# Relu out of zeroed PSUM rows and positions in eight transfers in the prologue; the fold of two weight matrices and two more units moved to the end of the pair loop

## The chip, the cores and the metric

One core of one Trainium2 chip. The metric is device time in microseconds (us), the median of several executions. The kernel before takes 2534.7 us (median of the six runs measured beside the changed kernel, 2533.2 to 2537.5; 2536.1 over the first three of them, which the prediction uses).

The engines are called by their names or by the profile's: TensorE is PE, VectorE is DVE, ScalarE is ACT, GpSimd is POOL, SyncE is SP; SPq and ACTq are the transfers that SyncE and ScalarE issue.

## The reference, cut to what matters

```python
# x, v: (4, 12544, 128); pos_emb: (12544, 64); w1: (64, 64); w2: (64, 128)
h_filt = (np.maximum(pos_emb @ w1, 0.0) @ w2) * np.exp(-0.01 * pos)[:, None]
y = causal convolution along the sequence of (x * v) with h_filt     # by an FFT of 2 * 12544
attn = x * y
# feed-forward on all 4 * 12544 rows; moe_w1..3: (128, 768), moe_w_out: (768, 128)
h = np.maximum(np.maximum(attn @ moe_w1, attn @ moe_w2), attn @ moe_w3)
out = h @ moe_w_out
```

The kernel takes the FFT as matrix products: first stages over "units" of channels (transpose, matmul against a small table; 32 units a batch), then second and inverse stages over 45 pairs of frequencies. The first maxout weight is taken out of the maximum: `max(a, b, c) = a + max(0, b - a, c - a)`, and the `a` part becomes one matrix, `lin = w1 w_out`, built by six "folds".

## The kernel before: the parts that the change and the argument touch

In time order: a prologue (positions, relu, filter's first stage, batch 0's units), a loop over the 45 pairs for batch 0, its drain, then 4 x 32 feed-forward tiles of six hidden blocks each. Beside the tiles of one batch runs the convolution of the next, dealt out over that batch's 192 hidden blocks ("slots").

```python
    def mlp_out(i):                      # prologue: relu times window, four operations a group
        ps = hidden.pop(i)
        v = ps[:].rearrange("n (r t f) -> n r f t", r=2, t=8)
        for h in range(2):
            n = slice(64 * h, 64 * h + HH)
            for r in range(2):
                nc.vector.scalar_tensor_tensor(
                    out=hs[n, :, r, 8 * i:8 * i + 8], in0=v[n, r], scalar=0.0,
                    in1=winr[n, r, None, 8 * i:8 * i + 8].to_broadcast([HH, FO, 8]),
                    op0=ALU.max, op1=ALU.mult)
# ... (cut)
    def conv_steps(b, done, lag):        # where each step of the next batch goes, in slots
        # ... (cut)
        per_pair = 172 / (NK + 0.95 * (NU - done))
        for u in range(done, NU, 2):
            s = (u - done) * 0.95 * per_pair + 6
            # ... (cut: load, product, transposes and first-stage groups of unit u)
        s0 = int((NU - done) * 0.95 * per_pair) + 7
        for g in range(NK):
            s = s0 + int(g * per_pair)
            at(s - 6, g_load, g)
            at(s + lag[4], g_third, b, g)      # lag = (1, 2, 3, 4, 5)
            at(s, g_second, g)
            at(s + lag[0], g_butterfly, g)
            at(s + lag[1], g_swap, g)
            at(s + lag[1], g_re, g)
            at(s + lag[2], g_im, g)
            at(s + lag[3], g_unfold, g)
# ... (cut)
    def up(i, f):                        # one hidden block: pa -> ScalarE relu, pb -> VectorE max
        rhs = gs[i][:]
        h = hp.tile([P, N], FP32, tag="hid", name="hid")
        pa = hps.tile([P, 512], FP32, tag="hps", name="pa")     # pa and pb share 2 buffers
        halves_mm(pa[:, 0:N], w_sb[1][:, f * P:(f + 1) * P], rhs, True, True)
        nc.scalar.activation(h[:], pa[:, 0:N], Relu)
        pb = hps.tile([P, 512], FP32, tag="hps", name="pb")
        halves_mm(pb[:, 0:N], w_sb[2][:, f * P:(f + 1) * P], rhs, True, True)
        nc.vector.tensor_tensor(out=h[:], in0=h[:], in1=pb[:, 0:N], op=ALU.max)
        return h
# ... (cut)
    EARLY = 4                            # units of batch 1 that the pair loop takes
    for s in range(NK + 3):
        # ... (cut: third, second, swap, filter, products of the pairs in flight)
        if folded is not None:
            folded()
            folded = None
        if 2 <= s < 2 + NF:
            folded = fold(s - 2)         # transpose, copy; the matmul follows a step later
    nc.scalar.copy(lin[:], pl[:, 0:D])
# ... (cut)
            beside = conv_steps(b + 1, EARLY if b == 0 else 0, (1, 2, 3, 4, 5))
```

## Time and profile before

| Stage of the kernel before, from its trace | us |
|---|---|
| start to the first loop step (prologue) | 129.1 |
| loop and drain, to the first tile's matmul | 198.8 |
| tiles of batch 0, beside the convolution of batch 1 | 580.0 |
| tiles of batch 1 | 587.5 |
| tiles of batches 2 and 3 | 1038.8 |
| span | 2534.1 |

A batch is counted from the first matmul of its first tile to that of the next batch.

### The profile page before, as it was taken

How to read it: one execution, taken by the hardware profiler on the slowest of the kernel's cores; microseconds unless marked ns; L12 is line 12 of the kernel's file. 1: busy time of each engine (PE TensorE's matmuls, PEld its weight loads, DVE VectorE, ACT ScalarE, POOL GpSimd, SP SyncE). 2: the span in 40 equal slices, each digit the busy share in tenths (PEclk: the TensorE clock that was granted, in tenths of full speed). 3: DMA queues.
4: the chain of work that ended last, by engine and by line, in shares of the span. 5: the costliest groups of instructions: out<-in, count | busy, mean ns of one | idle time of the engine just before them, and what ended most of it. 6: DMA issues, size and time to landing. Idle time of an engine off the chain costs nothing. (4 is left out here: it accounts for less than half of the span.)

```text
span 2534.1 us, 62487 instructions
## 1 busy us (share of the span) xinstructions
PE 2490.4 (98%) x26369; PEld 1512.8 (60%) x26369; DVE 1269.3 (50%) x2512; ACT 1041.5 (41%) x1976; POOL 68.5 (3%) x121
## 2 busy tenths in 40 slices
PE   7999999999999999999999999999999999999999
PEld 6988755565655555656566556655666654444444
DVE  5578833346666633336666733334766642222222
ACT  1688823334444423334444433333544432222222
POOL 2022200000000000000000000000000000000000
PEclk8999999999999999999999999999999999999999
DMA  6778854458787644457888834446888842222221
GB/s 137 196 215 273 251 115 107 95 143 227 211 226 211 174 105 96 100 134 181 229 215 229 224 91 107 101 95 182 222 235 223 231 115 52 62 56 56 59 53 35
DMA packets 428462, 384.51 MB, mean 152 GB/s; under 512 B 291358, under 2 KB 338197, under 8 KB 428053
## 3 DMA queue, kind: packets, MB, share of 16 engines
q1 hardware_dynamic: 305216, 290.84, 45.9%
q10 hardware_dynamic: 117653, 74.73, 10.1%
q0 software_dynamic: 5312, 14.95, 2.1%
q8 instruction: 206, 3.38, 0.6%
q14 instruction: 75, 0.61, 0.1%
HBM read 295.73 MB, written 84.67 MB: 150 GB/s over the span
## 5 line engine op out<-in xcount | busy, mean ns | idle before, releaser
L472 DVE TENSOR_TENSOR hid<-hid,pb 128x392 f32<-128x392 f32 x768 | 431.5, 562 | 775.1 <-PE pb L126 671.6
L469 ACT ACTIVATE hid<-pa 128x392 f32<-128x392 f32 x768 | 382.4, 498 | 713.5 <-PE pa L126 653.4
L126 PE MATMUL pa<-gt,w_sb 128*64 128x392 f32 x3072 | 641.0, 496 | 13.0 <-ACT hid L469 11.5
L126 PE MATMUL pb<-gt,w_sb 128*64 128x392 f32 x3072 | 636.1, 493 | 1.0 <-DVE hid L472 1.0
L126 PE MATMUL ops<-hid,wo_sb 128*64 128x392 f32 x3072 | 635.7, 492 | 0.1
L126 PEld LDWEIGHTS pb<-gt,w_sb 128*64 128x64 f32 x3072 | 217.7, 136 | 290.3 <-issue 206.4
L126 PEld LDWEIGHTS ops<-hid,wo_sb 128*64 128x64 f32 x3072 | 219.7, 137 | 286.2 <-issue 285.5
L126 PEld LDWEIGHTS pa<-gt,w_sb 128*64 128x64 f32 x3072 | 192.5, 137 | 150.1 <-issue 99.5
L135 PEld LDWEIGHTS ps<-f,uT 98*64 98x64 f32 x4096 | 183.7, 138 | 61.7 <-issue 58.2
L377 DVE TENSOR_TENSOR xt<-xt,ht 128x512 f32<-128x512 f32 x180 | 124.4, 691 | 186.1 <-ACT xs L372 124.9
L126 PEld LDWEIGHTS yps<-f,zt 90*64 90x64 f32 x4096 | 188.5, 136 | 48.0 <-issue 45.6
L126 PEld LDWEIGHTS ps<-ab,wt 128*64 128x64 f32 x2880 | 165.6, 137 | 55.5 <-issue 31.4
L400 ACT COPY zs<-ps 128x512 f32<-128x512 f32 x180 | 105.7, 587 | 225.1 <-PE ps L126 215.2
L135 PE MATMUL ps<-f,uT 98*64 98x90 f32 x4096 | 195.5, 242 | 1.3 <-ACT zs L400 0.7
L126 PE MATMUL yps<-f,zt 90*64 90x98 f32 x4096 | 195.3, 247 | 0.6 <-DMA zt<-zd 0.6
L126 PE MATMUL ps<-ab,wt 128*64 128x128 f32 x2880 | 190.3, 274 | 3.9 <-DVE ab L388 3.0
L126 PE MATMUL ps<-spec,wt 128*64 128x128 f32 x2880 | 187.8, 273 | 0.0
L126 PEld LDWEIGHTS ps<-spec,wt 128*64 128x64 f32 x2880 | 164.9, 137 | 17.5 <-issue 17.5
L460 DVE TENSOR_TENSOR gt<-yps,xT 128x392 f32<-128x392 f32 x128 | 72.5, 566 | 161.0 <-PE yps L126 143.7
L371 ACT ACTIVATE xs<-xt 64x512 f32<-64x512 f32 x180 | 113.1, 628 | 79.8 <-DVE xt L152 47.9
L139 ACT COPY spec<-ps 128x360 f32<-128x360 f32 (+1 forms) x128 | 69.9, 546 | 168.2 <-PE ps L135 167.9
L388 DVE TENSOR_TENSOR ab<-xt 128x256 f32<-128x256 f32 x360 | 135.7, 418 | 1.6
(67 smaller groups left out, 1592.7 us busy)
## 6 DMA issues: line engine op xcount, KB each, us to landing
wt<-wt_const SPq DMA_DIRECT2D x135, 512.0 KB, 4.7
ht<-hd SPq DMA_DIRECT2D x270, 256.0 KB, 5.7
zd<-zs ACTq DMA_DIRECT2D x180, 256.0 KB, 4.9
zt<-zd SPq DMA_DIRECT2D x128, 360.0 KB, 5.9
ut<-in_xr_dram SPq DMA_DIRECT2D x128, 196.0 KB, 3.7
ut<-in_vr_dram SPq DMA_DIRECT2D x128, 196.0 KB, 4.0
xT<-in_x_dram SPq DMA_DIRECT2D x512, 49.0 KB, 4.2
out_dram<-ot ACTq DMA_DIRECT2D x128, 196.0 KB, 3.5
```

The costliest lines, as they stand in the source:

```text
L126: nc.tensor.matmul(out[64 * h:64 * h + 64], lhsT[:, 64 * h:64 * h + 64], rhs, start=start, stop=stop, skip_group_check=True)
L135: nc.tensor.matmul(ps[64 * c:64 * c + 64, 256 * i + r * N1:256 * i + (r + 1) * N1], a[:, r, :], table[:, c * N1:(c + 1) * N1], start=(i % ...
L139: copy(dst, ps[:].rearrange("p (s m) -> p s m", m=256)[:, :, 0:2 * N1].rearrange("p s (r k) -> p k r s", r=2))
L371: nc.scalar.mul(xs[0:64], xt[64:128], -1.0)
L377: nc.vector.tensor_tensor(out=xt[:], in0=xt[:], in1=hts[g][:, 0], op=ALU.mult)
L388: nc.vector.tensor_tensor(out=ab[:, :, q, :], in0=y[:, :, 0, :], in1=y[:, :, 1, :], op=op)
L400: nc.scalar.copy(zs[:].rearrange("p k f -> p (k f)"), ps[:])
L460: nc.vector.tensor_tensor(out=g[:], in0=ps[:, 0:N], in1=xTs.pop(i)[:].rearrange("d p n -> d (p n)"), op=ALU.mult)
L469: nc.scalar.activation(h[:], pa[:, 0:N], Relu)
L472: nc.vector.tensor_tensor(out=h[:], in0=h[:], in1=pb[:, 0:N], op=ALU.max)
```

## The change

Its intent: let the positions land sooner, halve VectorE's relu work (one operation over 105 rows in place of two over 41 and 41, with the rows between zeroed in PSUM), take the six folds out of loop steps that they made longer, and let the loop do two more units of batch 1, so that fewer are left beside the feed-forward tiles. The diff, cut to its core:

```diff
-    nc.gpsimd.memset(hs[32:64].rearrange("n f r t -> n (f r t)"), 0.0)
+    pms = [fps.tile([P, 1024], FP32, name=f"pm{i}", bufs=1) for i in range(2)]
+    for pm in pms:
+        nc.vector.memset(pm[32:64], 0.0)
 # ... (cut: positions in eight transfers on two queues; first units ahead of the raw weights)
-        for _ in range(10):
+        for _ in range(16):                      # warm-up rounds
 # ...
     def mlp_out(i):
-        ps = hidden.pop(i)
-        v = ps[:].rearrange("n (r t f) -> n r f t", r=2, t=8)
-        for h in range(2):
-            n = slice(64 * h, 64 * h + HH)
-            for r in range(2):
-                nc.vector.scalar_tensor_tensor(
-                    out=hs[n, :, r, 8 * i:8 * i + 8], in0=v[n, r], scalar=0.0,
-                    in1=winr[n, r, None, 8 * i:8 * i + 8].to_broadcast([HH, FO, 8]),
-                    op0=ALU.max, op1=ALU.mult)
+        v = pms[i % 2][0:64 + HH].rearrange("n (r t f) -> n r f t", r=2, t=8)
+        for r in range(2):
+            nc.vector.scalar_tensor_tensor(
+                out=hs[:, :, r, 8 * i:8 * i + 8], in0=v[:, r], scalar=0.0,
+                in1=winr[:, r, None, 8 * i:8 * i + 8].to_broadcast([64 + HH, FO, 8]),
+                op0=ALU.max, op1=ALU.mult)
 # ... (cut)
-    EARLY = 4
+    EARLY = 6
+    loads = dict(zip((NK - 16, NK - 14, NK - 12, NK - 9, NK - 8, NK - 4), range(EARLY)))
+    muls = dict(zip((NK - 13, NK - 11, NK - 10, NK - 5, NK - 3, NK - 1), range(EARLY)))
+    turns = {NK - 9: 0, NK - 4: 2}
     for s in range(NK + 3):
 # ...
-        if folded is not None:
-            folded()
-            folded = None
-        if 2 <= s < 2 + NF:
-            folded = fold(s - 2)
+        # (cut: loads, products and transposes of units from these tables)
+        if NK <= s < NK + 2:
+            for v in range(4):
+                u_first(2 * (s - NK) + v // 2, v % 2, nc.scalar.copy)
+    for f in range(NF):
+        folded = fold(f)
+        if f == 0:
+            u_turn(4)
+            u_turn(5)
+        folded()
     nc.scalar.copy(lin[:], pl[:, 0:D])
+    for u in (4, 5):
+        for h in range(2):
+            u_first(u, h)
 # ... (cut: the first-stage groups beside the first tile's loads go)
```

`conv_steps` isn't in the diff. It reads `EARLY` as its `done`.

More of the change, by code (lines that the diff above doesn't have):

```diff
@@ L224 @@
     sml = fin.enter_context(tc.tile_pool(name="sml", bufs=1))
-    fps = fin.enter_context(tc.tile_pool(name="fps", bufs=4, space=PSUM))
+    mps = ExitStack()
+    fps = mps.enter_context(tc.tile_pool(name="fps0", bufs=4, space=PSUM))
     specH = pin.tile([P, N1, 2, FO], FP32, name="specH")
@@ L244 @@
     nc.vector.memset(win[:], 0.0)
-    nc.gpsimd.memset(hs[32:64].rearrange("n f r t -> n (f r t)"), 0.0)
+    pms = [fps.tile([P, 1024], FP32, name=f"pm{i}", bufs=1) for i in range(2)]
+    for pm in pms:
+        nc.vector.memset(pm[32:64], 0.0)
     for h in range(2):
         nc.scalar.dma_start(w1_sb[64 * h:64 * h + 64], w1[:, :])
-        (nc.scalar if h else nc.sync).dma_start(
-            pos[64 * h:64 * h + 64], posT[:, h * HH * P:(h + 1) * HH * P])
+    cuts = (0, 11, 21, 31, HH)
+    for j, (lo_, hi_) in enumerate(zip(cuts, cuts[1:])):
+        for h in range(2):
+            (nc.scalar if (h + j) % 2 else nc.sync).dma_start(
+                pos[64 * h:64 * h + 64, lo_ * P:hi_ * P],
+                posT[:, (h * HH + lo_) * P:(h * HH + hi_) * P])
     for h in range(2):
@@ L262, in warm_up @@
     def warm_up():
-        ps = fps.tile([P, 1024], FP32, tag="cv", name="pw")
-        for _ in range(10):
+        ps = fps.tile([P, 1024], FP32, tag="cv", name="pw", bufs=2)
+        for _ in range(16):
             halves_mm(ps[:, 0:256], warm[:, 0:P], warm[:], True, True)
     def window_back():
-        pw = fps.tile([P, 1024], FP32, tag="cv", name="pw")
+        pw = fps.tile([P, 1024], FP32, tag="cv", name="pw", bufs=2)
         nc.tensor.transpose(pw[:, 0:64 + HH], win[:], eye[0:64 + HH, 0:64 + HH])
@@ L278, in window_back @@
                           w2_in[lo_:lo_ + FO].rearrange("f (g c) -> f c g", c=GC), m)
-    hidden = {}
     def mlp_in(i):
-        ps = fps.tile([P, 1024], FP32, tag="cv", name="pm")
+        ps = pms[i % 2]
         for r in range(2):
@@ L292, in mlp_in @@
                         skip_group_check=True)
-        hidden[i] = ps
     def mlp_out(i):
-        ps = hidden.pop(i)
-        v = ps[:].rearrange("n (r t f) -> n r f t", r=2, t=8)
-        for h in range(2):
-            n = slice(64 * h, 64 * h + HH)
-            for r in range(2):
-                nc.vector.scalar_tensor_tensor(
-                    out=hs[n, :, r, 8 * i:8 * i + 8], in0=v[n, r], scalar=0.0,
-                    in1=winr[n, r, None, 8 * i:8 * i + 8].to_broadcast([HH, FO, 8]),
-                    op0=ALU.max, op1=ALU.mult)
+        v = pms[i % 2][0:64 + HH].rearrange("n (r t f) -> n r f t", r=2, t=8)
[4 more added lines that the diff above has]
+                op0=ALU.max, op1=ALU.mult)
     NU = NG
@@ L334, in u_turn, with u_first @@
                        ps[0:NB, :].rearrange("n (s t r) -> n s r t", s=4, r=2))
-    def u_first(u, h):
+    def u_first(u, h, copy=None):
         t = uts[u] if h == 0 else uts.pop(u)
@@ L340, in u_first @@
         first_halves(ps, [t[:, at % 8 + j] for j in range(2)], f1[:], spec[:, :, :, at:at + 2],
-                     copies[h])
+                     copy or copies[h])
     def g_load(g):
@@ L524 @@
     warm_up()
-    raws.append(load_raw(*jobs[0], nc.gpsimd))
-    raws.append(load_raw(*jobs[1], nc.gpsimd))
-    for u in range(6):
+    raws.append(load_raw(*jobs[0], nc.sync))
+    u_load(0, 0)
+    u_load(0, 1)
+    raws.append(load_raw(*jobs[1], nc.sync))
+    for u in range(2, 6):
         u_load(0, u)
-    for i in range(10):
+    for i in range(9):
         if i < 8:
@@ L533 @@
             window_back()
-        if i > 1:
-            mlp_out(i - 2)
+        if i:
+            mlp_out(i - 1)
+    mps.close()
+    fps = fin.enter_context(tc.tile_pool(name="fps", bufs=4, space=PSUM))
     for f in range(0, FO, 4):
@@ L640 @@
             g_butterfly(s)
-        u, odd = divmod(s - NK + 16, 2)
-        if 0 <= u < EARLY and not odd:
-            u_load(1, u)
-        if 2 <= u < EARLY + 2 and odd:
-            u_mul(u - 2)
-        if u in (4, 6) and not odd:
-            u_turn(u - 4)
-            u_turn(u - 3)
-        if folded is not None:
-            folded()
-            folded = None
-        if 2 <= s < 2 + NF:
-            folded = fold(s - 2)
+        if s in muls:
+            u_mul(muls[s])
+        if s in turns:
+            u_turn(turns[s])
+            u_turn(turns[s] + 1)
+        if s in loads:
+            u_load(1, loads[s])
+        if NK <= s < NK + 2:
[7 more added lines that the diff above has]
+        folded()
     nc.scalar.copy(lin[:], pl[:, 0:D])
+    for u in (4, 5):
+        for h in range(2):
+            u_first(u, h)
     pro.close()
@@ L680 @@
             t_load(*tiles[1])
-            for u in range(EARLY):
-                for h in range(2):
-                    u_first(u, h)
             t_last(tiles[0])
```

## The prediction

> **What bounds the kernel now.** I read the page first, then busy time by windows of 20 us, then the timelines of the parts that the change touches. The page says that nearly all of the span is TensorE work back to back:
>
> ```profile
> PE 2490.4 (98%) x26369; PEld 1512.8 (60%) x26369; DVE 1269.3 (50%) x2512; ACT 1041.5 (41%) x1976; POOL 68.5 (3%) x121
> PE  7999999999999999999999999999999999999999
> ```
>
> Only the first slice (63 us each) is not full. So from 331 us on, where the feed-forward tiles begin, PE is the limit, and there a change is worth exactly the PE work it takes away. The change acts in three places: the prologue (0 to 129 us), the loop over 45 frequency pairs (129 to 312) and its drain (312 to 331). The timeline of the prologue, put together from the engines' answers:
>
> ```profile
> 3.88 11.33 ACTq L254 DMA_DIRECT2D eye<-eye_const  x1
> 20.78 0.47 ACTq L257 DMA_DIRECT2D w_in<-in_w_dram  x1
> 23.56 0.40 ACTq L260 DMA_DIRECT2D f<-f_const  x1
> 23.99 1.28 ACT L271 ACT_TABLE_LOAD   x1 [23.99 <-DMA w_in<-in_w_dram]
> 26.09 0.27 ACT L274 COPY winr<-pw 105x128 f32<-105x128 f32 x1 [0.56 <-PE pw L272]
> 26.47 20.93 DVE L301 SCALAR_TENSOR_TENSOR spec<-pm,winr 41x512 f32<-41x512 f32 x32 [25.19 <-ACT winr L274]
> 17.44 5.63 PE L288 MATMUL pm<-w_sb,specH 64*41 64x64 f32 x126 [6.67 <-DMA specH<-in_pos_emb_dram]
> 47.05 5.80 PE L135 MATMUL ps<-f1h,spec 105*64 105x90 f32 x96 [5.85 <-DVE spec L301]
> 53.80 5.18 PE L135 MATMUL ps<-f1h,spec 105*64 105x90 f32 x128
> ```
>
> The reader is to see a chain: ScalarE issues its last transfer at 23.56, only then loads its table and copies the window (winr at 26.36); VectorE then works 20.93 us without a gap on 32 relu-times-window operations; TensorE, done with its matmuls at 41.2, waits 5.85 us for it. The first 96 matmuls after that wait take 5.80 us where 128 take 5.18 a little later: the clock had dropped. The windows show it (columns: stretch, length, busy PE, PEld, DVE, ACT, POOL, granted clock, DMA share, GB/s):
>
> ```profile
> 46.00:50.00 4.00, 2.95 (x38) 2.87 (x40) 3.88 (x11) 0.13 (x1) 0.00 (x0) 0.50 0.02 4
> 160.00:244.00 84.00, 84.00 (x1199) 70.45 (x1200) 73.39 (x147) 72.33 (x128) 21.96 (x42) 1.00 0.87 265
> ```
>
> The second line is the loop: PE full, DVE and DMA both at 87%. Its end and the drain, on PE and SyncE:
>
> ```profile
> 280.22 0.38 SPq L314 DMA_DIRECT2D ut<-in_xr_dram  x1
> 285.54 1.09 PE L126 MATMUL ps<-ab,wt 128*64 128x128 f32 x16 [0.75 <-DMA wt<-wt_const]
> 287.44 0.66 PE L592 MATMUL gps<-wt,specH 128*64 128x128 f32 x8 [0.81 <-DMA wt<-wt_const]
> 318.53 1.21 PE L126 MATMUL ps<-ab,wt 128*64 128x128 f32 x16 [2.08 <-DVE ab L388]
> 320.43 6.83 PE L135 MATMUL ps<-f,uT 98*64 98x90 f32 x128 [0.69 <-ACT zs L400]
> 327.86 1.57 PE L126 MATMUL yps<-f,zt 90*64 90x98 f32 x32 [0.60 <-DMA zt<-zd]
> ```
>
> After the last inverse matmul (318.53) the result goes to DRAM and back, and 327.86 is when it lands; PE fills that gap with the eight first-stage groups of batch 1.
>
> **What the Trainium skill says.** "TensorE: Matmul & The Clock Gate", Part 1: the clock is halved after an idle window of about 3.4 us and needs such a window of work to return. The trace agrees: 5.85 us idle, then clock 0.50. "VectorE: DVE Perf Modes", on reducing along the partition axis: "each of the 128 partition lanes is an independent pipeline". So one operation on 105 rows should cost what one on 41 rows does, 20.93/32 = 0.65 us; the trace has products on 128x512 from SBUF at 0.69, which fits. "DMA: Bandwidth & Descriptors", Issuing engines are not separate DMA queues: spreading issues only saves issue time. The trace agrees: from 5 to 10 us the two queues took 69.6% and 32.5% of the engines, together full, at 210 GB/s. Same page, Why a DMA increments its semaphore by 16: the number of engines must divide the row count, so, 41 being prime, the two 41-row window transfers run on one engine. No view names the engine, but the window and, behind it, the identity land last (23.7 us), long after the positions (17.3).
>
> **The change, part by part.**
> *Positions and queue order.* 2.69 MB at about 215 GB/s (from the 210 and 228 of 5 to 13 us) take 12.5 us from the first byte at 2.2: all positions at 14.7 instead of 17.3, as the maxout weights and units no longer compete. The cuts run over row blocks and every matmul group needs all of them, so splitting starts nothing earlier. What the order of the built program changes more is ScalarE's issue chain. Each transfer from SyncE or ScalarE waits for the one eight before it; in the old order the w2 load waits for a unit load (landed 20.8), in the new one for a piece of raw weights (about 15.5), and the chain's last gate is the second window piece. I put that at 18 to 20 (82 packets behind the positions; before, the last 41 took about 1.7 us, my estimate from the issues that waited for the two pieces, 21.4 and 23.2). Then 0.8 us of issue, 1.28 of table load, about 1.1 to the window copy: winr near 22.6 instead of 26.4.
> *Relu out of zeroed rows.* 32 operations become 16: 16 x 0.65 = 10.5 us. VectorE stops being the limit, TensorE takes over: two groups before the window, then six of 64 matmuls, at 32 ns warm or 43 cold (62 and 47 in 2 us), some 4.5 us of it cold: 13.8 us. With 1.4 for the first relu pair and 1.4 for the last: winr + 16.6 = 39.2 for the first filter quad, against 47.05. That is -7.8. TensorE idles only 1.5 us there, so the 96 matmuls run at 40.5 ns, 3.9 instead of 5.8: -1.8. Two PSUM memsets and six warm-up rounds lie before the positions land and cost nothing; GpSimd's 6.92 us memset goes. Sum -9.5. The following stages shift as they are: unit loads come free with PE's progress.
> *Fold out of the loop.* Steps with a fold start 4.54 us apart, steps without 3.93: 6 x 0.61 = -3.7.
> *Unit loads.* In the old order the fourth unit load stands at SyncE before the transposes that free its buffer (issued only at 280.22); table loads behind it come late and one step takes 5.89, 1.9 lost. The new order puts that load behind the transposes. But two more units are loaded in the loop (0.8 MB on queues 87% full) and two more products run (0.5 us each on DVE). I take -1.0 net.
> *Drain.* The eight first-stage groups move before the last two inverse groups. PE has about 3.6 us of gaps there and gets 8 x 0.65 = 5.2: the last inverse group slips about 2.2 us, ScalarE doing all eight copies of 0.48. After it, the DRAM round trip is 9.3 us to the first tile (318.53 to 327.86), and PE fills it with the transposes of two units (1.0), six folds in series (0.33 transpose, 0.27 copy, 0.39 matmul, hops: about 1.05 each) and four more groups (2.6): about 10, so the tile starts some 0.7 later still. Less about 0.7 for a clock that stays up (0.59 at 330 to 334 before): +2.2.
> *Batch 1.* Two units less beside the feed-forward tiles: 1.01 us of transposes for a pair and 4 x 0.62 for groups, PE-bound: -3.5.
> Sum: -9.5 -3.7 -1.0 +2.2 -3.5 = -15.5; 2536.1 becomes 2521, 0.6% less.
>
> **The rivals.**
> 1. The window stays the gate. If the one-engine window pieces and ScalarE's issue chain end at 24 as before, winr stays at 26.4 and PE, not VectorE, follows it by 16.6: the prologue gives only about 4 + 1.8. For it: it was the last thing to land before. Against: SyncE's unit loads now wait for the identity, and GpSimd's queue is empty then. Total -11.8, 2524.3.
> 2. The serial fold in the drain costs more than the loop saved: six PE to ACT to PE round trips at 1.5 us and a half clock through thin PE work would push the first tile by 4 us more, and 2525 results. Against: nothing in that chain holds the first tile's load; it waits only for its own stores.
> 3. The extra loads starve the loop: the two extra units are 0.8 MB, 3 us at the 265 GB/s of the loop, on queues with 13% free. If the old stall merely moves, -1.0 becomes +2: 2524.
> 4. Better: the window at 20 us and no stall left in the loop: 2516.
> A slowdown over 2% needs 50 us and nothing in the change reaches the stages that are 2200 us long except by taking work out; a gain of over 2% would need more than the whole prologue's waiting.
>
> **Range and chances.** The prologue term is -6 to -11.5, loop -2 to -6, drain 0 to +5, batch 1 firm; they are nearly independent, so I take 2514 to 2529 about 2521. Faster by over 2%: 0.01; within: 0.985; slower: 0.005.
>
> **What would show it.** Right: 16 relu operations of 0.65 us with gaps, waiting for PE; first filter quad near 39 us at clock 1.00; no loop step above 5.3 us and none at 4.54; first feed-forward matmul near 317 to 320 instead of 330.81; the distance from there to the end some 3.5 us shorter. Wrong: a relu on 105 rows that takes much over 0.65; winr at 26; a table-load wait of over 2 us in the loop; the zt load issued late behind the fold; a first tile that waits for PE more than 2 us after its data landed.

## More of the kernel before

TensorE's waits while it works on the tiles of batch 0 (columns: the waiting engine, tile and line; what it waited for; us in total, times, longest):

```profile
PE pa L126 <- ACT hid L469: 4.8, 12, 0.6
PE pa L126 <- DVE gt L460: 1.4, 1, 1.4
PE yps L126 <- DMA zt<-zd: 0.6, 1, 0.6
```

The first line is the one to keep in mind: twelve times in 192 slots TensorE waits until ScalarE has made the relu of an earlier block. It is under 1% of the stage, so the stage looks bound by TensorE alone.

Part of batch 0's first tile ran at half clock (columns: stretch, length, busy time of PE, PEld, DVE, ACT and POOL with instruction counts, granted clock, DMA share, GB/s):

```profile
330.70:334.10 3.40, 3.29 (x10) 1.19 (x12) 0.35 (x2) 0.50 (x1) 0.00 (x0) 0.50 0.77 171
```

That tile took 12.54 us; in the changed kernel, where no half clock falls into it, it takes 10.44.

## The result, and the profile after

| | median us | runs | range |
|---|---|---|---|
| before | 2534.7 | 6 | 2533.2 to 2537.5 |
| changed | 2531.4 | 6 | 2529.0 to 2535.6 |

The ratio is 0.9988, 95% interval 0.9975 to 1.0001: the same within 2%, 3.3 us between the medians. Ratios here and below are the mean time of one kernel's fast runs over that of the other's of the same rounds, so they are not quite the ratio of the medians that are quoted. The prediction was 2521.0 with 2514 to 2529, so it missed: a gain of 3 us in place of 15.

The profiled run of the changed kernel was its fastest of six (span 2527.3), and that of the kernel before (2536.0) lies 1.3 us above its median, so the two profiles differ by more than the medians do. A second profile, from the repeat that is told under the experiments, has a span of 2529.2, nearer to the median; both are given where it matters. Busy time of the engines, from the page:

```profile
PE 2491.1 (99%) x26393; PEld 1512.2 (60%) x26393; DVE 1259.7 (50%) x2494; ACT 1042.2 (41%) x1980; POOL 57.5 (2%) x112
```

TensorE is as busy as before, though work was taken from its path. The stages, by the same cuts as above:

| us | before | changed | repeat | predicted difference |
|---|---|---|---|---|
| to the first loop step | 129.1 | 122.8 | 123.4 | -9.5 |
| loop and drain, to the first tile | 198.8 | 197.9 | 198.7 | -2.5 |
| tiles of batch 0 | 580.0 | 581.3 | 582.1 | -3.5 |
| tiles of batch 1 | 587.5 | 586.2 | 586.1 | 0 |
| the rest | 1038.8 | 1039.0 | 1038.9 | 0 |

**Prologue.** The timeline (columns: start us, length us, engine, line, operation, output and inputs, count, in brackets the idle time before and what ended it):

```profile
16.32 6.03 PE L294 MATMUL pm<-w_sb,specH 64*41 64x64 f32 x128 [5.61 <-DMA back<-back_const]
19.39 1.28 ACT L278 ACT_TABLE_LOAD   x1 [19.39 <-DMA w_in<-in_w_dram]
23.43 0.27 ACT L281 COPY winr<-pw 105x128 f32<-105x128 f32 x1 [0.56 <-PE pw L279]
23.73 2.48 DVE L302 SCALAR_TENSOR_TENSOR spec<-pm,winr 105x512 f32<-105x512 f32 x4 [20.26 <-ACT winr L281]
25.07 15.23 PE L294 MATMUL pm<-w_sb,specH 64*41 64x64 f32 x384 [1.68 <-DVE spec L302]
33.37 1.29 DVE L302 SCALAR_TENSOR_TENSOR spec<-pm,winr 105x512 f32<-105x512 f32 x2 [1.03 <-PE pm L294]
41.89 3.94 PE L135 MATMUL ps<-f1h,spec 105*64 105x90 f32 x96 [1.60 <-DVE spec L302]
66.04 2.41 PE L135 MATMUL ps<-f,uT 98*64 98x90 f32 x57 [1.45 <-issue]
```

A relu operation on 105 rows takes 1.29 / 2 = 0.65 us, as one on 41 rows did, and VectorE now waits for TensorE: that part came as intended. The last line is a stop of TensorE with no wait in sight (1.45 us, "issue"). The stretches of half clock fall differently in the repeat, where the six groups keep the clock and the filter's matmuls lose it:

```profile
25.64 14.16 PE L294 MATMUL pm<-w_sb,specH 64*41 64x64 f32 x384 [1.68 <-DVE spec L302]
41.39 5.59 PE L135 MATMUL ps<-f1h,spec 105*64 105x90 f32 x96 [1.59 <-DVE spec L302]
```

**Drain.** TensorE's timeline:

```profile
308.26 1.05 PE L126 MATMUL ps<-ab,wt 128*64 128x128 f32 x16
312.94 0.44 PE L126 MATMUL pl<-wo_sb,w1t 128*64 128x128 f32 x4 [0.41 <-ACT w1t L589]
316.54 4.30 PE L135 MATMUL ps<-f,uT 98*64 98x90 f32 x64
320.68 1.52 PE L126 MATMUL yps<-f,zt 90*64 90x98 f32 x32
```

The first line is the last inverse group, ten microseconds earlier than before. Then come the folds one after the other, five of the six with some 0.4 us of waiting for ScalarE's copy in the middle; then 64 matmuls in 4.30 us, 67 ns each, where 128 took 6.83 us, 53 ns, in the kernel before; then the first tile, which waits for no data.

**Tiles of batch 0.** TensorE's waits there, to be read beside the three lines of the kernel before:

```profile
PE pa L126 <- ACT hid L470: 5.0, 14, 0.4
PE pb L126 <- DVE hid L473: 3.3, 12, 0.5
PE pa L126 <- DVE gt L461: 0.7, 1, 0.7
PE pb L126 <- ACT hid L470: 0.6, 1, 0.6
```

The second line is new: twelve waits for VectorE's maximum, which frees the PSUM buffer that `pb` needs. Where the time of this stage went can be worked out from the trace by adding up, for each kind of matmul, the time from its start to the start of the next matmul (so a wait counts with the kind that stood before it):

| us from start to start, tiles of batch 0 | before | changed |
|---|---|---|
| first-stage groups of units (`ps<-f`) | 35.9 | 33.3 |
| unit transposes (`pst`) | 14.1 | 13.1 |
| `pa` | 127.7 | 132.9 |
| `pb` | 125.7 | 125.9 |
| `ops` (both kinds) | 152.9 | 153.2 |
| `yps` | 45.1 | 44.3 |
| second and inverse groups | 78.6 | 78.6 |
| sum | 580.0 | 581.3 |

The two units did leave: 2.6 + 1.0 = 3.6 us, to a tenth the predicted 3.5. But `pa` takes 5.2 us more, with the same number of matmuls; by this way of counting 3.9 of them are the waits of `pb` that follow it (3.3 and 0.6). And the sums hide a part: the kernel before has 2.1 us of half clock and waiting in its first tile that the changed one has not. One such place (all engines, the changed kernel):

```profile
571.89 0.58 ACT L401 COPY zs<-ps 128x512 f32<-128x512 f32 x1 [3.05 <-PE ps L126]
572.96 0.63 ACT L372 ACTIVATE xs<-xt 64x512 f32<-64x512 f32 x1 [0.48 <-ACT zs L401]
573.60 0.62 ACT L373 COPY xs<-xt 64x512 f32<-64x512 f32 x1
574.24 0.37 ACT L157 COPY eo<-ps 128x256 f32<-128x256 f32 x1
574.51 0.50 ACT L470 ACTIVATE hid<-pa 128x392 f32<-128x392 f32 x1
575.06 0.88 PE L126 MATMUL pa<-gt,w_sb 128*64 128x392 f32 x4 [0.37 <-ACT hid L470]
578.12 0.88 PE L126 MATMUL pb<-gt,w_sb 128*64 128x392 f32 x4 [0.21 <-DVE hid L473]
```

ScalarE gets four convolution copies in one slot (0.58 + 0.63 + 0.62 + 0.37 = 2.2 us: the inverse group of one pair, the swap of another, the second stage of a third), so the relu of a block whose `pa` matmuls began at 572.55 and took 0.83 starts only at 574.51; TensorE waits 0.37 us for it, and two blocks later, because VectorE has fallen behind too, 0.21 us more.

### The profile page after: what moved, and what is told of

Same layout as the page of the kernel before. It is cut to its first block, busy times and chain, and to the rows that moved or that the text cites. A ratio compares the mean times of both kernels' runs of the same rounds, so it can differ in the third digit from the quotient of the medians.

```text
span 2527.3 us, 62508 instructions
## 1 busy us (share of the span) xinstructions
PE 2491.1 (99%) x26393; PEld 1512.2 (60%) x26393; DVE 1259.7 (50%) x2494; ACT 1042.2 (41%) x1980; POOL 57.5 (2%) x112
## 3 DMA queue, kind: packets, MB, share of 16 engines
q0 software_dynamic: 5056, 14.16, 1.9%
## 5 line engine op out<-in xcount | busy, mean ns | idle before, releaser
L126 PEld LDWEIGHTS ps<-spec,wt 128*64 128x64 f32 x2880 | 164.6, 137 | 14.9 <-issue 14.7
```

The costliest lines, as they stand in the source:

```text
L126: nc.tensor.matmul(out[64 * h:64 * h + 64], lhsT[:, 64 * h:64 * h + 64], rhs, start=start, stop=stop, skip_group_check=True)
```

## The experiments

All outputs are right. The kernel before ran beside them in each of three sets: 2535.1 (experiments 1 to 4), 2534.8 (6 to 9) and 2534.8 (5 and 10 to 12).

**1. The changed kernel again.** No edit.

> The changed kernel once more, unchanged: how far one profile and one set of rounds can be trusted. Its first profile gave 2527.3 us against 2534.1, but that run was the fastest of six, and the medians were 3.3 us apart. If the difference between profiles is partly chance (where the clock's half-speed stretches fall), the stages before the first feed-forward matmul (322.87 in the first profile) will move by 1 to 3 us; the span of batch 0 from its first tile to that of batch 1 (581.3 us) should repeat within 1 us. Ratio to before 0.997 to 1.000.

Measured: 2531.0, ratio 0.9988 (0.9975 to 1.0). The miss stands, and the second profile has the same stages (column "repeat" above). The 0.8 us more in batch 0 lie in one tile, the 24th, before which ScalarE took 1.22 us to issue a transfer in place of 0.40; experiment 4 comes back to this.

**2. The old places in the tiles of batch 0.** Theory: `done` is also a divisor of the schedule. With 4 units done early, `per_pair` is 172 / (45 + 0.95 x 28) = 2.402 slots; with 6 it is 172 / (45 + 0.95 x 26) = 2.468, and the pairs start at slot 67 in place of 70. So the change also moved all 45 pairs, and with them ScalarE's crowded slots. This kernel takes the two units out and leaves every other step where it was:

```diff
-        per_pair = 172 / (NK + 0.95 * (NU - done))
+        base = 4 if done else 0
+        per_pair = 172 / (NK + 0.95 * (NU - base))
         for u in range(done, NU, 2):
-            s = (u - done) * 0.95 * per_pair + 6
+            s = (u - base) * 0.95 * per_pair + 6
 # ...
-        s0 = int((NU - done) * 0.95 * per_pair) + 7
+        s0 = int((NU - base) * 0.95 * per_pair) + 7
```

> The changed kernel, but the steps of batch 1's convolution keep the slots that they had before (the grid for four finished units; the slots of units 4 and 5 stay empty). Theory A: the new grid (2.468 slots a pair instead of 2.402) packs more copies of ScalarE and products of VectorE into single slots, and TensorE's 3.6 us of saved work are given back as waits for the relu and the maximum. Then batch 0's span (579.9 before, 581.3 after) becomes 579.9 - 3.6 = 576.3, within 1 us, and the whole 4 to 5 us less than the changed kernel. Rival B: ScalarE and VectorE limit this stage whatever the slots, so saved TensorE work turns into waiting in any case: 580 to 581, and no change of the whole.

Measured: 2522.2, ratio 0.9949 (0.9936 to 0.9963): 8.8 us better than the changed kernel beside it, twice what was expected. The tiles of batch 0 take 572.8 us, 8.5 less than in the changed kernel's first profile. TensorE's waits there:

```profile
PE pa L126 <- ACT hid L471: 3.9, 11, 0.5
PE pa L126 <- DVE gt L462: 0.7, 1, 0.7
```

The waits of `pb` are gone. The start-to-start times: `pa` 126.6 (132.9 in the changed kernel), `ops` 151.5 (153.2), units 46.5 as in the changed kernel.

**3. The new places in the kernel before.** The converse: only the pairs of batch 1 move to the spacing of 2.468 and the start at 67, and the units, still 28, are squeezed in before them.

```diff
-        per_pair = 172 / (NK + 0.95 * (NU - done))
+        base = 6 if done else 0
+        per_pair = 172 / (NK + 0.95 * (NU - base))
+        per_unit = per_pair * (NU - base) / (NU - done)
 # ... (units spaced by per_unit; s0 with base)
```

> The kernel before, with only the pair steps of batch 1 set on the new grid (2.468 slots a pair from slot 67), its 28 units pressed into the slots ahead of it. No work is taken out or added. Theory A: batch 0's span grows from 579.9 to 584 or 585, from waits of pb for the maximum and pa for the relu. Rival B: it stays within 1 us of 579.9.

Measured: 2541.8, ratio 1.0028 (1.0015 to 1.0041), 6.7 us slower than before. The tiles of batch 0 take 584.2, 4.2 more (from the second tile on, without the half clock of the kernel before, 6.3 more), and the same waits appear that the changed kernel has:

```profile
PE pa L126 <- ACT hid L471: 5.1, 14, 0.4
PE pb L126 <- DVE hid L474: 3.3, 12, 0.5
```

So the places of the pairs alone make these waits; they lie from slot 77 on, where no unit is left. Their slots show how (a slot here is that of the block whose relu comes late). A tile has six slots. In the kernel before, nine of the twelve waits (slots 80, 92, 104 and so on to 176) are 12 apart and so at the same place of every second tile (place 2, counted from 0), because five pairs take 5 x 2.402 = 12.01 slots; the other three (145, 157, 169) are 12 apart too. In the changed kernel five pairs take 12.34, and the waits drift over all places (77, 82, 92, 102, 107, 114 ...). After a wait at the old place 2 (92, 134, 176) no wait of `pb` follows; after one at places 4 and 5 a wait of `pb` comes two slots later in six of seven cases.

**4. The prologue alone.** The changed kernel with the old loop, drain and `EARLY = 4`.

```diff
-    EARLY = 6
+    EARLY = 4
 # ... (loop, fold and first tile as in the kernel before)
```

> The kernel before with only the prologue of the change (positions in eight pieces, relu from zeroed rows, queue order, 16 warm-up rounds). The change's first loop step came 6.3 us sooner than before (122.8 against 129.1). If the parts add, this kernel has its first loop step at 122 to 124, the loop and the rest as before (batch 0's span 579.9), and is 5 to 7 us faster than before. If the prologue's gain in the first profile was partly luck with the clock: 3 to 4 us.

Measured: 2528.1, ratio 0.9971 (0.9958 to 0.9983), 7.0 us faster. The first loop step is 4.3 us earlier than before (124.7), not 9.5. This profile also has a stop of TensorE, 1.81 us, followed by 3.4 us of half clock. The other gain lies where the prologue has no business: the tiles of batch 0 take 578.1 (-1.9) and those of batch 1 586.1 (-1.4, two waits of `pa` fewer). Every kernel with the old prologue has 586.9 to 587.5 there, every one with the new prologue and the old places of batch 2's pairs 586.1 to 586.3. The trace shows what stood there. ScalarE issues the stores `zd<-zs` between its copies, and in the kernel before some of these issues took three times as long, so that the copies and the relu behind them came late; first the kernel before, then this one at the same slot:

```profile
775.74 1.22 ACTq L401 DMA_DIRECT2D zd<-zs  x1
```

```profile
770.80 0.40 ACTq L402 DMA_DIRECT2D zd<-zs  x1
```

The kernel before has four such issues in batch 0 (0.74 to 1.22 us; the median is 0.40) and three in batch 1, this one has one (1.05) and none. Three of the four stand at the slots 145, 157 and 169. Against experiment 8, which has none in batch 0, the tiles concerned are 2.7 us longer in the kernel before, 0.6 here and 1.2 in experiment 2. Why an issue takes longer isn't shown.

**5. The loop and the drain alone.** The kernel before with the changed loop, drain and `EARLY = 6`.

```diff
-    EARLY = 4
+    EARLY = 6
 # ... (loop, fold and first tile as in the changed kernel; old prologue)
```

> The kernel before with everything of the change but the prologue: fold and units 4 and 5 in the drain, the new order of unit loads, and the new slots. If the parts add, this is the whole change (-3 us) less the prologue (-7): about 3 to 4 us SLOWER than before, with the loop faster, the drain slower, and batch 0's span at 581 to 583 with 3.3 us of waits of pb for the maximum. Rival (the parts do not add, the new slots hurt only together with the new prologue's transfer order): 0 or faster.

Measured: 2537.5, ratio 1.0009 (0.9997 to 1.0022): no gain, or a loss of 2 us. Its batch 0 takes 581.4, as the changed kernel's does. So all that the change gains comes from the prologue, and the rest of it gives part of that back.

**6. The fold back in the loop** (from here on every edit is against the kernel of experiment 2).

```diff
-    for f in range(NF):
-        folded = fold(f)
-        if f == 0:
-            u_turn(4)
-            u_turn(5)
-        folded()
+        if folded is not None:
+            folded()
+            folded = None
+        if 2 <= s < 2 + NF:
+            folded = fold(s - 2)
+    u_turn(4)
+    u_turn(5)
```

> The kernel with the old slots, and the fold of w1 w_out put back into the third to eighth loop steps. Theory: the move of the fold gave nothing. Out of the loop it saves 6 x 0.61 = 3.7 us there, but in the drain it is a chain of 7.3 us that TensorE must finish before the first tile, whose data landed some 3 us earlier, and its thin work lets the clock drop. So from the first loop step to the first feed-forward matmul this kernel needs 200.9 us as with the fold in the drain (old_slots), within 1 us, with steps of 4.5 us in the loop and the first tile's matmul waiting for its data. Rival: the data were not there earlier (the tile waits for its transfer either way); then this kernel is 3 to 4 us slower, about 204.5.

Measured: 2522.9, ratio 0.9953 (0.994 to 0.9967), the same as experiment 2. Without the folds TensorE waits for the data in the drain:

```profile
320.92 2.20 PE L126 MATMUL yps<-f,zt 90*64 90x98 f32 x32 [3.34 <-DMA zt<-zd]
```

What the loop loses with the folds in it, the drain gets back: moving them is worth nothing by itself (loop 3.4 longer, drain 4.6 shorter). The pause of 3.34 us has a price further on, too: half clock from 321.7 to 328.5, which makes the first tile 13.14 us long in place of 10.44.

**7. The folds a step ahead.** The transpose of fold f+1 before the matmul of fold f, with the four first-stage groups between them, so that no fold waits for its copy.

```diff
-    for f in range(NF):
-        folded = fold(f)
-        if f == 0:
-            u_turn(4)
-            u_turn(5)
-        folded()
+    firsts = [(u, h) for u in (4, 5) for h in range(2)]
+    folded = fold(0)
+    u_turn(4)
+    u_turn(5)
+    for f in range(1, NF):
+        ahead = fold(f)
+        folded()
+        folded = ahead
+        if firsts:
+            u_first(*firsts.pop(0))
+    folded()
```

> The kernel with the old slots, fold in the drain, but each transpose goes ahead of the matmul of the fold before it and the four last first-stage groups stand between them, so that TensorE does not wait for ScalarE's copy. Theory: the drain is limited by TensorE's serial chain (11.4 us from the last inverse group to the first tile, of which 2.0 are waits for copies and 1.6 a half clock). Then that stretch falls to 8 to 9 us, where the data's landing limits it, and the whole by 2.5 to 3.5 us against old_slots. Rival (the landing of the first tile's data limits): no change.

Measured: 2522.8, ratio 0.9952 (0.9939 to 0.9964): no gain, a miss. The drain did shrink: from the last inverse group to the first tile 10.6 us, 13.4 in experiment 2. But TensorE now meets the data's arrival, and after the pause its clock is halved in the first tiles:

```profile
320.12 2.01 PE L126 MATMUL yps<-f,zt 90*64 90x98 f32 x32 [2.06 <-DMA zt<-zd]
322.88 1.57 PE L126 MATMUL pa<-gt,w_sb 128*64 128x392 f32 x4 [0.75 <-DVE gt L462]
```

Four `pa` matmuls take 1.57 us there and 0.88 in the changed kernel; half clock lasts from 321.1 to 327.9, and the tiles of batch 0 take 575.9 in place of 572.8.

**8. A third PSUM tile in the prologue,** so that TensorE doesn't wait for VectorE to empty one of two; and 24 warm-up rounds in place of 16, against the half clock of the first groups.

```diff
-    pms = [fps.tile([P, 1024], FP32, name=f"pm{i}", bufs=1) for i in range(2)]
+    pms = [fps.tile([P, 1024], FP32, name=f"pm{i}", bufs=1) for i in range(3)]
-        for _ in range(16):
+        for _ in range(24):
-    for i in range(9):
+    for i in range(10):
 # ... (window_back's two tiles become one; mlp_out(i - 2), pms[i % 3])
```

> The kernel with the old slots, with a third PSUM tile of zeroed rows for the relu units (one pw buffer instead of two) and 24 warm-up rounds instead of 16. Theory: the prologue's gain fell short because TensorE, now the limit there, ran its first two groups at half clock (5.97 us for 128 matmuls) and then waited 1.7 us for the first relu pair. Then the first filter quad comes at 38.5 to 39.5 instead of 41.9, groups of 64 take 2.33 us from the start, and the whole falls by 2 to 3 us. Rival: VectorE or the landing of the window sets it; then it stays at 41.5 or more.

Measured: 2517.3, ratio 0.993 (0.9918 to 0.9943), about 5 us faster than experiment 2. From the timeline:

```profile
16.25 6.13 PE L294 MATMUL pm<-w_sb,specH 64*41 64x64 f32 x128 [3.16 <-DMA back<-back_const]
23.36 14.16 PE L294 MATMUL pm<-w_sb,specH 64*41 64x64 f32 x384
39.11 3.94 PE L135 MATMUL ps<-f1h,spec 105*64 105x90 f32 x96 [1.59 <-DVE spec L302]
```

The third tile works as meant: the six groups run without a wait (14.16 us, 36.9 ns a matmul), and the first filter matmul comes at 39.1, 2.8 earlier. But the loop starts 6.3 us earlier than in experiment 2 (118.7 against 125.0), more than the third tile explains. TensorE's stop near 65 us, 2.05 us in experiment 2 and followed by half clock from 67.2 to 70.6, is almost gone here, though the table loads are issued as before and the transfer engines are full (1.04):

```profile
60.76 1.17 PE L135 MATMUL ps<-f1h,spec 105*64 105x90 f32 x25 [0.20 <-issue]
58.00:62.00 4.00, 3.80 (x99) 3.63 (x95) 2.84 (x7) 2.14 (x4) 1.84 (x4) 1.00 1.04 276
```

The longer warm-up failed: it ended 3.16 us ahead of the first group, and that group's clock fell all the same (6.13 us for two groups, 6.03 before). The windows of that pause and of two stretches around the drain of the changed kernel show how (columns as above); first this kernel, then the changed one:

```profile
14.20:17.60 3.40, 1.34 (x32) 1.36 (x34) 0.00 (x0) 0.00 (x0) 0.00 (x0) 1.00 0.63 130
```

```profile
313.30:316.70 3.40, 2.17 (x21) 1.25 (x21) 0.00 (x0) 0.80 (x3) 0.00 (x0) 1.00 0.18 29
316.70:320.10 3.40, 3.40 (x52) 3.40 (x48) 0.53 (x1) 0.73 (x2) 0.00 (x0) 0.50 0.91 196
```

In neither of the two stretches ahead of a half clock was TensorE idle throughout: it was busy for 1.34 and for 2.17 of 3.40 us, and the next stretch ran at half clock all the same. The serial folds are thin enough work for that: in all seven profiles that have them in the drain (the changed kernel, its repeat, experiments 2, 5, 8, 9 and 10) the stretch with them is followed by half clock, and in experiments 11 and 12, where they are not serial, none follows. But TensorE's busy time alone doesn't decide it: in experiment 4 the stretch from 309.5 to 312.9 us held 1.97 us of work, and the next one ran at full clock. How thin is too thin can be narrowed down from the traces. In each of the fourteen profiles all changes of the granted clock lie whole multiples of 3.413 us apart. Cut into windows at these times, the first 345 us of each show 44 windows at full clock that were followed by half clock; none held more than 2.18 us of TensorE work. Every full-clock window with less than 1.40 us was followed by half clock; between 1.40 and 2.18 both happened.

**9. Table loads later.** Theory: the stop of TensorE near 65 us is its instruction stream coming late, because six table loads for the loop (128 rows each) are issued at about that time and fill the transfer engines. This kernel issues them after unit 16.

```diff
-    wf = {g: load_dir(g, 0) for g in range(3)}
-    wi = {g: load_dir(g, 1) for g in range(3)}
 # ... in the loop over units:
+        if u == 16:
+            wf = {g: load_dir(g, 0) for g in range(3)}
+            wi = {g: load_dir(g, 1) for g in range(3)}
```

> The kernel with the old slots, with the first six table loads (1.5 MB) issued nine unit pairs later. In every kernel TensorE stands still once near the first unit group, with no wait that the profile shows: 0.66 us before, 1.45, 0.90 and 2.05 in kernels with the new prologue, about 1.6 us after a 16 KB instruction fetch landed. Theory: that fetch comes late because the six table loads and the raw weights fill the queues just then. Then the stop shrinks to under 0.5 us here and the clock does not drop at 67 us. Rival: the stop has nothing to do with the queues' load: it stays at 1 to 2 us.

Measured: 2520.9, ratio 0.9946 (0.9934 to 0.9959); the loop starts 2.0 us earlier than in experiment 2. The same matmuls and the same 4 us in experiment 2 and in this kernel, a timeline line and a window of each:

```profile
66.64 4.06 PE L135 MATMUL ps<-f,uT 98*64 98x90 f32 x57 [2.05 <-issue]
62.00:66.00 4.00, 2.59 (x67) 2.42 (x64) 2.98 (x8) 2.13 (x3) 0.61 (x2) 1.00 1.03 246
```

```profile
64.30 2.65 PE L135 MATMUL ps<-f,uT 98*64 98x90 f32 x64
62.00:66.00 4.00, 4.00 (x108) 4.00 (x106) 3.90 (x11) 2.53 (x4) 0.80 (x2) 1.00 0.34 101
```

With the transfer engines at 0.34 in place of 1.03 the stop is gone. In every other profile with the new prologue and the early table loads, but for experiment 8, it was between 0.90 and 2.05 us; in the kernels with the old prologue between 0.66 and 1.08. It ended 1.2 to 1.8 us after a 16 KB packet of the instruction queue had landed. That the stop is a wait for instructions is therefore supported by this run and by that order in time, not seen directly; and experiment 8 (0.20 us with the engines as full) shows that full engines alone do not make it.

**10. Old spacing in all batches.** If a spacing of 2.402 beats a drifting one, batches 2 and 3, spaced by 2.281 from slot 76 on, should gain by it too, with their units pressed into 70 slots.

```diff
-        base = 4 if done else 0
+        base = 4
         per_pair = 172 / (NK + 0.95 * (NU - base))
+        per_unit = per_pair if done else per_pair * (NU - base) / NU
```

> The kernel with the old slots for batch 1, and the same pair grid (2.402 slots a pair from slot 70, units pressed into the slots ahead) for batches 2 and 3 too. Theory: five pairs in twelve slots, two tiles of six, lock the crowded slots to one place in the tile (slot 2 of every second tile, the only place where old_slots waits); 2.468 and 2.281 let them drift through all six places, and where they meet the tile's own copies TensorE waits longer. Then the spans of batches 1 and 2 fall from 586.1 by 2 to 4 us each, the whole by 4 to 8 against old_slots. Rival (the count of crowded slots is what costs: 12 at 2.281, 17 at 2.402, 20 at 2.468): the spans of batches 1 and 2 grow by 1 to 2 us each.

Measured: 2524.4, ratio 0.9955 (0.9942 to 0.9967), so not faster than experiment 2: the theory's forecast missed. Batches 1 and 2 take 586.1 and 587.7 us (586.1 both in experiment 2). Split at the fourteenth tile, the later part is shorter (344.8 and 346.4 against 348.0) and the earlier one longer (241.3 against 238.1), but that is work that crossed the cut, because the pairs now start six slots sooner: the earlier part holds 48 second-stage matmuls (2.6 us) and 16 of a unit (0.6) more. So the pressed units cost nothing, and the spacing that stays in step with the tiles gains nothing; the 1.6 us in batch 2 go with two of ScalarE's long issues (1.16 us each).

**11. The parts that helped, together:** experiments 2, 7, 8 and 9 in one kernel.

```diff
+        base = 4 if done else 0                                   # 2
+    pms = [... for i in range(3)]                                 # 8
+        if u == 16: wf, wi = ...                                  # 9
+        ahead = fold(f); folded(); folded = ahead; u_first(...)   # 7
```

> Old slots, third PSUM tile of zeroed rows and 24 warm-up rounds, table loads later, fold pipelined in the drain. three_rows alone ran at 0.993 of before; the later tables add up to 1 us, the pipelined fold nothing (its gain went to a later half clock). 2515 to 2518 us.

Measured: 2511.6, ratio 0.9904 (0.9889 to 0.9919). It beats both kernels: 23 us faster than before, 20 than the changed one. The single gains against experiment 2 (2522.2) were 4.9, 1.3 and -0.6 and would give 2516.6. What is gained beyond that shows in the drain:

```profile
314.79 1.57 PE L126 MATMUL yps<-f,zt 90*64 90x98 f32 x32
317.13 0.88 PE L126 MATMUL pa<-gt,w_sb 128*64 128x392 f32 x4 [0.76 <-DVE gt L462]
```

The order of experiment 7 takes 8.65 us here from the last inverse group to the first tile, with no wait for data and no half clock: the data were there when TensorE was. The traces tell why they came sooner than in experiment 7. The first tile's load is issued when the last store of the inverse group has landed, 3.6 us after that store's issue in experiment 7 and 1.9 here. In experiment 7 a 16 KB packet of the instruction queue ran from 312.17 to 313.47, just behind the store's issue (311.56), and the store's last packets came after it; here there was none. All six runs with such a packet just behind the store's issue, the changed kernel among them, have 3.5 to 4.2 us, the other eight 1.9 to 2.2. That the packet holds the store up is concluded from this order; no run isolates it. Experiment 8, with the serial folds, shows what their order is worth once the data come early: they landed at 313.4, and the first tile began at 318.2.

**12. The same with the old spacing in all batches** (edit of experiment 10 on top).

```diff
-        base = 4 if done else 0
+        base = 4
+        per_unit = per_pair if done else per_pair * (NU - base) / NU
```

> The same with the locked grid for all batches: what locked_all gains over old_slots (theory: 4 to 8 us) comes on top, 2508 to 2513 us; by the rival of locked_all 2518 to 2521.

Measured: 2515.3, ratio 0.992 (0.9906 to 0.9933), some 4 us slower than experiment 11. Batches 1 and 2 take 587.0 and 587.5 us (586.1 and 586.2), with six of ScalarE's long issues (0.64 to 0.94 us); the rest I haven't taken apart. The old spacing is not worth having in the later batches.

## Why the prediction was wrong, point by point

**The step that failed** is the one under "Batch 1": "Two units less beside the feed-forward tiles ... PE-bound: -3.5", with "batch 1 firm" in the range. The work left by the predicted amount (3.6), but the stage became 1.4 us longer (2.1 in the repeat), although its first tile had lost 2.1 us of half clock and waiting: 7.1 us stand against the two. The step held that stage to be worth exactly the TensorE work in it, and did not follow `EARLY` into `conv_steps`, where it divides 172 slots among the pairs. The runs show what stood in its place: moving only the pairs to the new places costs the kernel before 4.2 us in that stage (6.3 from the second tile on) and 6.7 in all; leaving them at the old ones saves the changed kernel 8.5 in that stage and 8.8 in all, and gives 2522.2, within the predicted range. The cost is TensorE waiting for ScalarE and then VectorE where several pairs' copies fall into one slot. By the prediction's own test, from the first feed-forward matmul to the end should be 3.5 us shorter; it was 2203.3 before and is 2204.4.

The size differs, 4.2 us in one kernel and 8.5 in the other, mostly because of two things that are not the places: the half clock and the wait in the first tile of the kernel before (2.1), and ScalarE's long issues (2.7 in the kernel before, 1.2 in experiment 2, nothing in the two kernels with the new places). Without them the new places cost 9.0 us in the kernel before (584.2 against 575.2) and 9.7 in the changed one (581.3 against 571.6), my estimate from the times of the tiles. The same figures account for all of the 7.2 us that separate experiment 2's batch 0 from that of the kernel before: 3.6 of work, 2.1 and 1.5. What stays open is what makes a place costly, the drift against the tiles or the number of crowded slots; experiment 10 gives no support to the drift, since batches spaced by 2.281 drift as well and gained nothing from 2.402.

**Prologue, -9.5: right in kind, too large.** The first loop step came 6.3 us sooner (5.7 in the repeat). Term by term: the positions, put at 14.7, landed at 16.1 and let the first matmuls begin at 16.3; the window copy starts at 23.4, 2.7 earlier than before (26.1), with its end predicted at 22.6 and measured at 23.7, because ScalarE was ready at 20.7 but TensorE turned the window only at 22.3, after its first two groups (6.03 us, partly at half clock); the six groups took 15.2 in place of the 13.8 worked out, with 3.4 us of them at half clock (26.5 to 29.9), while in the repeat, at full clock, they took 14.2; the first filter matmul is at 41.9, not 39.2. The 13.8 itself comes from a misread count and a slip: the 62 and 47 matmuls in 2 us include those that only reach into the window (54 of the 62 started in it; a warm group takes 2.33 us, 36.4 ns a matmul, not 32), and 32 and 43 ns with 4.5 us cold would give 13.5. The filter matmuls took 3.94 us, predicted 3.9, but that was luck: in the repeat the same wait of 1.6 us was followed by half clock, and they took 5.59. Relu at 0.65 on 105 rows is right. A term was missing: the stop of TensorE near 65 us, 1.45 us here and 0.66 in the kernel before. Together: -5.2 to the first filter matmul, -1.9 for its clock, +0.8 for the stop, makes -6.3.

**Fold out of the loop and unit loads, -4.7: right, slightly small.** From the first loop step to the last, 179.3 us became 173.5, so -5.8. No step with a fold's 4.54 us and no stall of 5.9 was left, and the waits for table loads in the loop (1.6 us before) are gone. The loads of two more units did not starve the loop: the third rival fell.

**Drain, +2.2: too small, +4.9.** From the start of the last loop step to the first tile 19.5 us became 24.4. The last inverse group slipped by 1.8, for which 2.2 was reckoned. Two transposes and six folds took 7.3 us (309.24 to 316.54), as reckoned (1.0 and six times 1.05). What was missing is the last inverse group's own 1.0 us, for the 9.3 were counted from its start, and a half clock: the four groups took 4.3 where 2.6 was reckoned. The prediction took 0.7 off "for a clock that stays up": the half clock of the first tile did go, but another came ahead of it (316.7 to 320.1). The first tile's data landed at 319.27 and waited 1.4 us for TensorE. Loop and drain together: -5.8 + 4.9 = -0.9 in the first profile.

**The rivals.** The first (window still the gate) fell: the window copy ended at 23.7, not 26.4. The second was right about the half clock after thin work, but a fold took 1.11 us and not 1.5, and the drain came 2.7 over the forecast, not 4. The third fell, as told. The fourth fell with the size of the prologue. None of the four was about the tiles, where the loss was.

Even with the drain and the prologue as measured, -7.2 to the first tile, a batch 0 at -3.5 would have given 2525.4 (2536.1 - 7.2 - 3.5), in the range: it is the places of the pairs that put the result outside it.

## What to carry to other kernels

When a change takes work out of a schedule that is computed, follow the changed constant into every formula that reads it: here the number of units done early also spaced 45 pairs, and moving those cost more than the two units were worth (8.5 against 3.6 us). A stage in which one engine is 98% busy is bound by that engine only as long as its feeders keep their places; look for the slot in which the lightly loaded engine (here ScalarE, 41%) gets several stages' work at once. When two profiles of a stage are compared, look first for what fell into one of them only: here a half clock and a few long issues made 4.2 us of a cost of 9. Changes that gain nothing alone, as the folds in a better order did, should be tried again once what hides them (a wait, a dropped clock) is gone.

## What the Trainium skill lacked or had wrong

- "Runtime: NRT & Kernel Launch", Instruction fetch mechanics, has the cost of crossing a 16 KiB block of instructions as "mostly hidden". Here TensorE stopped for up to 2.05 us, waiting for nothing that the profile shows, 1.2 to 1.8 us after a packet of that size had landed, with the transfer engines full (1.03); with them at 0.34 it did not stop, but in experiment 8 it stopped for only 0.20 with them full (1.04). The page doesn't say when the fetch shows, nor that it may stand in the way of a store (landed 3.5 to 4.2 us after its issue with such a packet just behind the issue, 1.9 to 2.2 without; argued from the order in time).
- "TensorE: Matmul & The Clock Gate", Part 1, has the clock halved after an idle window of about 3.4 us; of frequent short pauses it says that they do it too, but not how thin the work must be. The half-clock stretches here last 3.41 us or a multiple of it, as the page says of windows, but the window ahead of one need not be idle: in fourteen profiles up to 2.18 us of TensorE work in it were followed by half clock, less than 1.40 always, more than 2.18 never. Warming up does not help if it ends early: a pause of 3.16 us was enough.
- No page that I found treats the cost of bunching: four ScalarE copies in one slot (2.2 us) make TensorE wait 0.37 us on an engine that is 41% busy, and moving them cost 4.2 and 8.5 us in a stage of 580.
